# Loading all queries and keys in runs of 512 bytes and reading even-odd queries with a strided pattern

## The chip, the cores and the metric

The kernel runs on one core of one Trainium2 chip. The metric is the device time of one execution in microseconds (us), the median of several. Executions are sorted into a fast and a slow state; the slow one is an execution more than 1.5% above the fastest of the same kernel. Each execution also has a granted clock, the mean share of full speed at which TensorE was let run; fast executions of one kernel can differ in it. Ratios are the mean time of one kernel's fast runs over that of the other kernel's fast runs of the same rounds, so they are not quite the ratio of the medians quoted beside them. The kernel before took 214.99 us (214.95 to 215.03, 2 runs) at first; on the chips of the later runs its median was 216.5 to 217.6 us, with single executions from 214.6 to 220.7. A difference below 1% is therefore only trusted here where an interval excludes it.

## The reference, cut to what matters

```python
# q, k, v: (4, 8, 768, 64), 0.1 * randn;  heads 0, 2, 6 see all earlier keys,
# the others see 4 "sink" keys and the last 64
scores = scale * np.matmul(q, k.transpose(0, 1, 3, 2))
scores = np.where(mask[None, :, :, :], scores, -1000000000.0)
a = np.exp(scores - np.max(scores, axis=-1, keepdims=True))
a = a / (np.sum(a, axis=-1, keepdims=True) + 1e-09)
attn = np.matmul(a, v)
# then, on x = attn as (3072, 512):  np.maximum(x @ w1, x @ w2) @ w_out
```

One thing matters for the experiments. A score is a sum of 64 products of two numbers of size 0.1, divided by 8: about 0.01. The softmax is nearly flat, so a kernel that uses the queries in a wrong order still passes the comparison with the reference. Several experiments below do that on purpose and were all reported as correct. So a correct result says nothing about the order of the queries; that has to follow from the indices.

## The kernel before

A small planner in Python lays out the order of all instructions from estimated durations; that order is then fixed. Work goes by 16 pairs of heads (`i`, four per batch). q and k of a pair are loaded, cast to bf16 by GpSimd (the first pair also by others), transposed by TensorE, and copied out of PSUM (in the trace of before the matmuls write the `bank` buffers there, and a copy of 128x768 out of one takes 0.54 to 0.56 us on VectorE when contiguous). Score matmuls (k is the stationary operand `lhsT`, whose load starts at 140.63 us in the rows quoted in the prediction, its first matmul at 140.64; q is the moving operand `rhs`, and the next start follows 0.11 to 0.12 us after 256 of its columns, 0.16 after 384), exponentials (ScalarE), masks (VectorE) and the product with v follow. The dense part of a finished batch fills the gaps of TensorE between the pairs of the next one.

The first four pairs (`i < HP`) load two neighbouring rows as one run of 512 bytes, so their transposes come out as all even positions, then all odd ones, in each block of 256. The copy puts them back in order by writing with a step of two elements:

```python
wide = which < 2 and i < HP
pat = ("h (m p r) d -> p h m (r d)", dict(p=128, r=2)) if wide else ("h (n p) d -> p h n d", dict(p=128))
...
if i < HP:                                     # copy of the transposed q or k
    o = o.rearrange("q (m p r) -> q m r p", p=128, r=2)
    in_ = in_.rearrange("q (m r p) -> q m r p", p=128, r=2)
ev(eng)(out=o, in_=in_)
...
for (j, q0, w, off) in segs:                   # the scores, two heads side by side
    for hh in range(2):
        nc.tensor.matmul(
            P["sc", i, st, hh][:, off:off + w],
            lhsT=kt[64 * hh:64 * hh + 64, j * 128:(j + 1) * 128],
            rhs=qt[64 * hh:64 * hh + 64, q0:q0 + w], ...)
...
batches = [[0, 1], [2, 3], [4, 5]] if i >= HP else [[s] for s in range(NS)]
cost = sum(f[1] for f in fns) / 2400.0         # what the planner thinks scores cost, us
```

## Time and profile before

| from the page of before | value |
|---|---|
| span of the profiled run | 214.5 us |
| TensorE busy | 190.4 us (89%) |
| VectorE, ScalarE busy | 128.9, 128.4 us (60% each) |
| packets of the loads and stores | 74,118, of them 62,832 under 512 bytes |
| score matmuls | 320 |

Most of the profile of before stands in the prediction. Two further rows of its page are needed for comparison: the busy share of TensorE in tenths, in 40 equal slices of the span, and its granted clock in tenths of full speed.

```profile
PE   0388786999999999999999989998999999699993
PEclk9999999699999999999999999999999999999999
```

TensorE is full from the eighth slice on, and its clock is granted at nine tenths or more but for one slice.

### The profile page before, as it was taken

How to read it: one execution, taken by the hardware profiler on the slowest of the kernel's cores; microseconds unless marked ns; L12 is line 12 of the kernel's file. 1: busy time of each engine (PE TensorE's matmuls, PEld its weight loads, DVE VectorE, ACT ScalarE, POOL GpSimd, SP SyncE). 2: the span in 40 equal slices, each digit the busy share in tenths (PEclk: the TensorE clock that was granted, in tenths of full speed). 3: DMA queues.
4: the chain of work that ended last, by engine and by line, in shares of the span. 5: the costliest groups of instructions: out<-in, count | busy, mean ns of one | idle time of the engine just before them, and what ended most of it. 6: DMA issues, size and time to landing. Idle time of an engine off the chain costs nothing.

```text
span 214.5 us, 4691 instructions
## 1 busy us (share of the span) xinstructions
PE 190.4 (89%) x1872; PEld 108.0 (50%) x1888; DVE 128.9 (60%) x297; ACT 128.4 (60%) x247; POOL 47.6 (22%) x59
## 2 busy tenths in 40 slices
PE   0388786999999999999999989998999999699993
PEld 0244554555655555546654646465555554454541
DVE  7799989944772577447746683667436651650800
ACT  2489698639873778468845686578458664102021
POOL 0155447154443231313112040401000000000000
PEclk9999999699999999999999999999999999999999
DMA  4999999999999899998911400210012011102112
GB/s 115 259 343 318 240 344 409 238 221 219 220 201 248 194 240 222 236 250 209 223 49 55 120 0 3 98 52 0 0 52 98 3 47 52 52 0 98 49 52 98
DMA packets 74118, 31.77 MB, mean 148 GB/s; under 512 B 62832, under 2 KB 68976, under 8 KB 74096
## 3 DMA queue, kind: packets, MB, share of 16 engines
q1 hardware_dynamic: 73952, 31.46, 60.4%
q8 instruction: 15, 0.25, 0.5%
q14 instruction: 7, 0.06, 0.1%
q10 hardware_dynamic: 144, 0.01, 0.0%
HBM read 25.17 MB, written 6.29 MB: 147 GB/s over the span
## 4 chain that ended last, share of the span: by engine, by line
PE 72%; DVE 19%; DMA 3%; ACT 2%; issue 2%; SPq 0%; ACTq 0%; DVEq 0%
PE bank_80 L504 12%; PE bank_79 L504 10%; PE bank_79 L477 6%; PE bank_73 L331 5%; PE bank_77 L390 5%; PE bank_80 L477 5%; PE bank_78 L390 4%; PE bank_75 L331 3%; DMA kn_84<-in_k_dram 3%; PE bank_80 L461 3%; DVE x_117 L412 3%; PE bank_74 L504 2%; PE bank_73 L504 2%; PE bank_79 L422 2%; DVE x_118 L412 2%
## 5 line engine op out<-in xcount | busy, mean ns | idle before, releaser
L477 PEld LDWEIGHTS <-wd_bf 128*128 128x128 bf16 x256 | 23.4, 97 | 16.2 <-issue 3.6
L504 PEld LDWEIGHTS <-gt_123 128*128 128x128 bf16 x96 | 9.4, 98 | 11.3
L504 PEld LDWEIGHTS <-gt_122 128*128 128x128 bf16 x96 | 9.4, 98 | 11.3
L343 ACT ACTIVATE at_101<-bank_73 128x512 bf16<-128x512 f32 x16 | 9.6, 599 | 4.2 <-PE bank_74 L331 4.2
L343 ACT ACTIVATE at_107<-bank_75,bias_j 128x512 bf16<-128x512 f32 x16 | 11.2, 703 | 0.3 <-PE bank_76 L331 0.3
L343 ACT ACTIVATE at_108<-bank_76,bias_j 128x512 bf16<-128x512 f32 x16 | 11.4, 710 | 0.0
L504 PE MATMUL bank_80<-wo_bf,gt_122 128*128 128x512 bf16 x48 | 11.3, 379 | 0.0
L343 ACT ACTIVATE at_104<-bank_76,bias_64 128x512 bf16<-128x512 f32 x16 | 11.2, 702 | 0.0
L343 ACT ACTIVATE at_109<-bank_73 128x384 bf16<-128x384 f32 x16 | 8.0, 498 | 5.3 <-PE bank_74 L331 5.3
L343 ACT ACTIVATE at_103<-bank_75,bias_64 128x512 bf16<-128x512 f32 x16 | 11.1, 694 | 0.0
L343 ACT ACTIVATE at_105<-bank_73 128x512 bf16<-128x512 f32 x16 | 9.7, 608 | 2.2 <-PE bank_74 L331 2.2
L331 PE MATMUL bank_73<-qt_97,kt_99 64*128 64x256 bf16 (+1 forms) x48 | 9.5, 277 | 1.3 <-DVE kt_99 L315 1.3
L331 PEld LDWEIGHTS <-kt_99 64*128 64x128 bf16 x160 | 5.9, 95 | 9.2 <-issue 6.2
L354 DVE TENSOR_TENSOR at_109<-at_109,msk 128x384 bf16<-128x384 bf16 x16 | 7.5, 469 | 5.1 <-ACT at_109 L343 5.1
L411 DVE RECIPROCAL rez_115<-bank_77 128x6 f32<-128x6 f32 x8 | 1.6, 194 | 14.9 <-PE bank_77 L390 14.9
L308 PE MATMUL bank_79<-ident,qb_90 128*128 128x128 bf16 x36 | 3.3, 234 | 7.4 <-ACT qb_90 L291 7.4
L294 POOL CAST vb_94<-vn_87 128x768 bf16<-128x768 f32 x6 | 5.0, 838 | 21.2 <-DMA vn_87<-in_v_dram 9.7
L343 ACT ACTIVATE at_106<-bank_74 128x512 bf16<-128x512 f32 x16 | 9.7, 608 | 0.0
L331 PEld LDWEIGHTS <-kt_100 64*128 64x128 bf16 x160 | 6.0, 94 | 7.3 <-issue 5.5
L343 ACT ACTIVATE at_102<-bank_74 128x512 bf16<-128x512 f32 x16 | 9.6, 598 | 0.0
L331 PE MATMUL bank_74<-qt_97,kt_99 64*128 64x256 bf16 (+1 forms) x48 | 9.3, 275 | 0.2 <-ACT at_106 L343 0.2
L504 PE MATMUL bank_79<-wo_bf,gt_123 128*128 128x512 bf16 x40 | 9.4, 379 | 0.0
(224 smaller groups left out, 539.7 us busy)
## 6 DMA issues: line engine op xcount, KB each, us to landing
w_f<-in_moe_w_dram SPq DMA_DIRECT2D x4, 1024.0 KB, 9.3
qn_81<-in_q_dram SPq DMA_DIRECT2D x6, 384.0 KB, 6.0
kn_84<-in_k_dram SPq DMA_DIRECT2D x6, 384.0 KB, 6.2
vn_87<-in_v_dram SPq DMA_DIRECT2D x6, 384.0 KB, 6.1
wo_f<-in_moe_w_out_dram SPq DMA_DIRECT2D x2, 1024.0 KB, 8.0
out_dram<-ot_124 SPq DMA_DIRECT2D x8, 256.0 KB, 2.2
out_dram<-ot_125 SPq DMA_DIRECT2D x8, 256.0 KB, 2.0
out_dram<-ot_126 SPq DMA_DIRECT2D x8, 256.0 KB, 2.0
```

The costliest lines, as they stand in the source:

```text
L294: ev(eng)(out=dst[:, :, :, 0:D], in_=src)
L308: nc.tensor.transpose(o[:, n * 128:(n + 1) * 128], src[:, n].rearrange("p h d -> p (h d)"), ident)
L331: nc.tensor.matmul(P["sc", i, st, hh][:, off:off + w], lhsT=kt[64 * hh:64 * hh + 64, j * 128:(j + 1) * 128], rhs=qt[64 * hh:64 * hh + 64, ...
L343: nc.scalar.activation(out=P["at", i, st, hh][:, 0:n], in_=P["sc", i, st, hh][:, 0:n], func=ACT.Exp, scale=scale, bias=bias)
L354: nc.vector.tensor_mul(out=at[:, 0:n], in0=at[:, 0:n], in1=mk)
L390: nc.tensor.matmul(po[:, qb_ * (D + 1):(qb_ + 1) * (D + 1)], lhsT=at[:, off + t * 128:off + (t + 1) * 128], rhs=vb[:, hh, j, :], start=(st ...
L411: nc.vector.reciprocal(out=rez, in_=po[:, :, D])
L412: nc.vector.tensor_tensor(out=P["x", b][:, :, h * D:(h + 1) * D], in0=po[:, :, 0:D], in1=rez.unsqueeze(2).to_broadcast([128, NB, D]), op=A ...
L422: nc.tensor.transpose(psb[:, n * 128:(n + 1) * 128], P["x", b][:, n, hp * 128:(hp + 1) * 128], ident)
L461: nc.tensor.matmul(P["mmM", c], lhsT=w2t[:, f, c * 128:(c + 1) * 128], rhs=wo_bf[:, f, :], start=(f == 0), stop=(f == FC - 1))
L477: nc.tensor.matmul(P["mmH", b, g, f][:, 0:GT], lhsT=wd_bf[:, c, f * 128:(f + 1) * 128], rhs=P["xt", b][:, c, g * GT:(g + 1) * GT], start=( ...
L504: nc.tensor.matmul(ps, lhsT=lhsT, rhs=rhs, start=(i == 0), stop=(i == KC + FC - 1))
```

## The change

The intent: halve the number of short load packets for all q and k rather than for the first four pairs, and not pay for it with a slow copy of q (in the trace of before such a copy takes 1.02 us on VectorE with a step of two, 0.56 contiguous). k is put in order by its copy, now in all 16 pairs. q is copied as it lies, even positions first, and the score matmul reads an even and an odd element in turn, 128 elements apart. A segment that begins at an odd block of 128 can't be described in one such pattern and is split. The x buffers become smaller, per pair; two switches for other variants are off.

```diff
-        wide = which < 2 and i < HP
+        wide = which < 2
...
-                if i < HP:
+                if which == 1:
                     o = o.rearrange("q (m p r) -> q m r p", p=128, r=2)
...
-            tops.append(P.add({"DVE": 0.56, "ACT": 0.72} if i >= HP else {"DVE": 1.02, "ACT": 1.02}, evac, ...
+            tops.append(P.add({"DVE": 0.56, "ACT": 0.72} if which == 0 else {"DVE": 1.02, "ACT": 1.02}, evac, ...
...
-                        nc.tensor.matmul(P["sc", i, st, hh][:, off:off + w], lhsT=..., rhs=qt[..., q0:q0 + w], ...)
+                        qv = qt[64 * hh:64 * hh + 64].rearrange("d (m r p) -> d m p r", p=128, r=2)
+                        while at0 < q0 + w:
+                            m, lo = at0 // 256, (at0 % 256) // 2
+                            if lo == 0 and q0 + w - at0 >= 256:
+                                n = (q0 + w - at0) // 256
+                                pieces.append((qv[:, m:m + n], 256 * n))
+                            else:
+                                pieces.append((qv[:, m, lo:lo + 64, :], 128))
+                            at0 += pieces[-1][1]
+                        for rhs, n in pieces:
+                            nc.tensor.matmul(P["sc", i, st, hh][:, o:o + n], lhsT=lhsT, rhs=rhs, ...)
...
-        "x": ring("x", 2, [128, NB, d_model], BF16),
+        "x": ring("x", 3, [128, NB, 128], BF16),
```

More of the change, by code (lines that the diff above doesn't have):

```diff
@@ L14 @@
 NEG = -30000.0
+QK_BY_DMA = 0
+X_BY_DMA = 0
 SWITCH = 0.1
@@ L302, in plan_pair, with move @@
             tb, tt = (("qb", "qt"), ("kb", "kt"))[which]
+            if QK_BY_DMA and i >= HP:
+                def move(eng, tb=tb, tt=tt):
+                    nc.sync.dma_start_transpose(
+                        out=P[tt, i].rearrange("p (n c) -> p n c", c=128),
+                        in_=P[tb, i].rearrange("p n h d -> p (n h d)"))
+                tops.append(P.add({"DMA": 0.9}, move, deps=[casts[which]], acq=[(tt, (tt, i))], rel=[(tb, i)],
+                                  prio=(0, i, which)))
+                continue
             def tr(eng, which=which, tb=tb):
@@ L317, in plan_pair @@
                       rel=[(tb, i)], prio=(1, i, which))
-            tops.append(P.add({"DVE": 0.56, "ACT": 0.72} if i >= HP else {"DVE": 1.02, "ACT": 1.02}, evac, deps=[t],
+            tops.append(P.add({"DVE": 0.56, "ACT": 0.72} if which == 0 else {"DVE": 1.02, "ACT": 1.02}, evac, deps=[t],
                               rel=[("mmT", i, which)], prio=(1, i, which)))
@@ L330, in fn @@
                     for hh in range(2):
-                        nc.tensor.matmul(
-                            P["sc", i, st, hh][:, off:off + w],
-                            lhsT=kt[64 * hh:64 * hh + 64, j * 128:(j + 1) * 128],
-                            rhs=qt[64 * hh:64 * hh + 64, q0:q0 + w],
-                            start=True, stop=True, skip_group_check=True)
+                        qv = qt[64 * hh:64 * hh + 64].rearrange("d (m r p) -> d m p r", p=128, r=2)
+                        lhsT = kt[64 * hh:64 * hh + 64, j * 128:(j + 1) * 128]
+                        pieces = []
+                        at0 = q0
+                        while at0 < q0 + w:
[6 more added lines that the diff above has]
+                            at0 += pieces[-1][1]
+                        o = off
+                        for rhs, n in pieces:
+                            nc.tensor.matmul(P["sc", i, st, hh][:, o:o + n], lhsT=lhsT, rhs=rhs,
+                                             start=True, stop=True, skip_group_check=True)
+                            o += n
             return fn, n, kind, segs
@@ L412, in fn @@
                 nc.vector.tensor_tensor(
-                    out=P["x", b][:, :, h * D:(h + 1) * D], in0=po[:, :, 0:D],
+                    out=P["x", i][:, :, hh * D:(hh + 1) * D], in0=po[:, :, 0:D],
                     in1=rez.unsqueeze(2).to_broadcast([128, NB, D]), op=ALU.mult)
             norms.append(P.add({"DVE": 0.62}, fn, deps=[last], rel=[("po", i, hh), ("rez", i, hh)],
-                               acq=[("rez", ("rez", i, hh))], use=[("x", ("x", b), H + HP)],
+                               acq=[("rez", ("rez", i, hh))], use=[("x", ("x", i), 3)],
                                prio=(0, i, hh)))
@@ L422, in xtr, with xmove @@
                 nc.tensor.transpose(psb[:, n * 128:(n + 1) * 128],
-                                    P["x", b][:, n, hp * 128:(hp + 1) * 128], ident)
+                                    P["x", i][:, n, :], ident)
         def xev(eng):
             ev(eng)(out=P["xt", b][:, hp, :], in_=P["mmX", i].bitcast(BF16)[:, 0:S])
-        t = P.add({"PE": 0.34}, xtr, deps=norms, acq=[("mm", ("mmX", i))], prio=(2, i, NS),
-                  use=[("x", ("x", b), H + HP), ("xt", ("xt", b), XT_USES)])
-        xt_ops[b, hp] = P.add({"DVE": 0.56, "ACT": 0.72}, xev, deps=[t], rel=[("mmX", i)],
-                              prio=(0, i, NS))
+        def xmove(eng):
+            nc.sync.dma_start_transpose(
+                out=P["xt", b][:, hp, :].rearrange("p (n c) -> p n c", c=128),
+                in_=P["x", i].rearrange("p n c -> p (n c)"))
+        if X_BY_DMA and i < len(pairs) - 1:
+            xt_ops[b, hp] = P.add({"DMA": 0.9}, xmove, deps=norms, prio=(0, i, NS),
+                                  use=[("x", ("x", i), 3), ("xt", ("xt", b), XT_USES)])
+        else:
+            t = P.add({"PE": 0.34}, xtr, deps=norms, acq=[("mm", ("mmX", i))], prio=(2, i, NS),
+                      use=[("x", ("x", i), 3), ("xt", ("xt", b), XT_USES)])
+            xt_ops[b, hp] = P.add({"DVE": 0.56, "ACT": 0.72}, xev, deps=[t], rel=[("mmX", i)], prio=(0, i, NS))
     wd_ops, wo_ops, wm_ops = [], [], []
```

## The prediction

Where the prediction speaks of a line, it means 16 bytes, eight neighbouring bf16 elements. That TensorE pays for a change of line, and the factors of two and four, were guesses of mine: the trace of before has no strided read to show them. The sweep e4 shows the step at that size (0.61 us a batch with two elements 4 apart in turn, 1.15 with two 8 apart), and e4 and e9 measure what a change costs. The lag of the second head is an estimate too, from 128 columns at the 2.4 per ns of the trace; after shows both heads' pieces starting within 0.01 us of each other.

> **What bounds the kernel now.** I read the busy table of the page first, then a table of three stretches of the span, then the order of TensorE's instructions in one steady stretch, then the group of the score matmuls and of the copies that follow the transposes of q and k.
>
> The stretches (columns: microseconds from the start, length, then busy time with the number of instructions for PE, PE weight loads, VectorE, ScalarE, GpSimd, then granted clock, DMA share, GB/s):
>
> ```profile
> 0.00:40.00 40.00, 25.82 (x327) 15.96 (x329) 35.70 (x87) 29.61 (x54) 16.24 (x23) 0.98 1.00 288
> 40.00:184.50 144.50, 138.50 (x1412) 78.83 (x1425) 83.66 (x194) 95.25 (x188) 31.39 (x36) 0.99 0.60 129
> 184.50:214.50 30.00, 26.12 (x137) 13.18 (x136) 9.49 (x17) 3.52 (x6) 0.00 (x0) 1.00 0.14 54
> ```
>
> There are three regimes. Up to 40 us VectorE is the full engine (35.70 of 40) and TensorE starves (25.82). From 40 to 184.5 us TensorE is busy 138.50 of 144.50, VectorE only 58% and ScalarE 66%: TensorE is the bound. The last 30 us are the dense work of the last batch, which neither q nor k touches. Busy time of pipelined matmuls overstates, so I check with column counts: the dense up products have 256 x 384 columns, the down products 192 x 512, the folded weight 32 x 512, the weight transposes 32 x 128, the q, k and x transposes 16 x 18 x 128, the score products 16 x 2688 per head (two heads side by side), attention times v 16 x 42 x 65. That is 98.3 + 147.5 + 16.4 + 4.1 + 36.9 + 43.0 + 43.7 = 389.9 thousand columns, at 2.4 columns per ns (the rate that the next view shows: 256 columns in some 0.11 us) 162 us of streaming in a span of 214.5. So from 40 us on every column that TensorE streams longer lengthens the kernel nearly one for one: its order of work is fixed by the program and nothing else is near full.
>
> The score matmuls in the steady stretch, with the waits in brackets:
>
> ```profile
> 140.63 0.33 PEld L331 LDWEIGHTS <-kt_99 64*128 64x128 bf16 x8 [0.42 <-issue]
> 140.64 0.28 PE L331 MATMUL bank_73<-qt_97,kt_99 64*128 64x256 bf16 x1
> 140.64 0.28 PE L331 MATMUL bank_74<-qt_97,kt_99 64*128 64x256 bf16 x1
> 140.76 0.27 PE L331 MATMUL bank_73<-qt_97,kt_99 64*128 64x256 bf16 x1
> 140.76 0.27 PE L331 MATMUL bank_74<-qt_97,kt_99 64*128 64x256 bf16 x1
> 140.87 0.32 PE L331 MATMUL bank_75<-qt_97,kt_99 64*128 64x384 bf16 x1
> 140.87 0.32 PE L331 MATMUL bank_76<-qt_97,kt_99 64*128 64x384 bf16 x1
> 141.03 0.22 PE L331 MATMUL bank_75<-qt_97,kt_99 64*128 64x128 bf16 x1
> ```
>
> Two heads (banks 73 and 74) start at the same instant[...]. The starts are 0.12, 0.11 and 0.16 us apart for 256, 256 and 384 columns, so q is read at full speed today: one column per 1/2.4 ns. The 0.27 us durations are latency, not spacing.
>
> The chip's queue for loads is full until about 105 us, but as a prefetch:
>
> ```profile
> DMA  4999999999999899998911400210012011102112
> DMA packets 74118, 31.77 MB, mean 148 GB/s; under 512 B 62832, under 2 KB 68976, under 8 KB 74096
> ```
>
> All of 40 to 105 us has both a full DMA and a full TensorE (19.2 of 20 us in each 20 us window), and in the list of TensorE's own waits no load of a later pair appears; the only long one is the 7.4 us of the very start.
>
> [...]a q or k copy takes 0.56 us on VectorE when contiguous and 1.02 when it writes with a step of two.[...]
>
> **The change part by part.**
>
> Loads. 12 pairs x 2 tensors go from 1536 runs of 256 bytes to 768 of 512: 18,432 packets fewer, so about 55,700 of 74,118. Loads from the fifth pair on land earlier and the full stretch of the queue ends perhaps 10 to 15 us earlier (24 loads, my estimate some 0.5 us each, as the 6.0 us to landing is three loads deep). On the end: nothing, because TensorE does not wait for them. The first four pairs, whose loads do matter, are wide already.
>
> Copies after the transposes. The first four q copies lose the step-two write: 4 x (1.02 - 0.56) = 1.8 us, or less where ScalarE does them (1.01 to 0.80). That lies in the stretch where VectorE is full: up to 1.5 us on the end. The other twelve k copies gain it: seen today as 8 on VectorE at about 0.55 and 4 on ScalarE at 0.82, so 8 x 0.46 + 4 x 0.20 = 4.5 us more, in a stretch where those engines are a third idle. On the end: 0 to 0.5.
>
> Score matmuls, number. Per head and pair today 10; segments that start at an odd block of 128 (queries from 128, 384 and again 384) fall into two pieces, so 13. That is 6 x 16 = 96 more matmuls and weight loads, with the same columns. Both pieces of one head are issued before the other head's, so the second head lags by one 128-column piece (0.053 us); the lag doesn't add up inside a batch of steps, so at most 2 to 3 times 0.053 a pair: 16 x 0.13 = 2 us at the most.
>
> Score matmuls, reading. The inner pattern is now two elements 128 columns (256 bytes) apart, then the next column[...]. If a new line costs twice the time of a column, the 2688 columns of a pair take 2.24 us rather than 1.12: 1.12 us more a pair, plus double the lag. Three pairs are through by 36 us, where TensorE has slack; thirteen count: 13 x (1.12 + 0.2) = 17 us. If it costs four times, 13 x 3.5 = 46 us.[...]
>
> Output buffers per pair rather than per batch (3 small ones instead of 2 large): freed by a transpose that follows within 2 us, so no new wait.
>
> Sum with the factor of two: 215.0 + 17 + 1 (lag and copies early) - 1.5 = 231.5; I put 231.
>
> **The rivals.** First: the strided read is free. Then 215.0 + 2 - 1.5 = 215.5, within 2%. [...]Second: a line costs four columns: some 262. [...]Third: the loads were the limit after all, and the kernel gains. For it: the DMA row of nines up to slice 19; against: the TensorE row of nines beside it. At most the 6 us of idle in the middle stretch could come back, and little of that is ascribed to loads: 210 to 213. Fourth: the k copies, 1.02 us in front of a pair's first score matmul, become a wait. Each pair's chain would lengthen by 0.46 us, but dense work is interleaved; 12 x 0.2 = 2.4 us at worst, so 217.
>
> **Range and chances.** I give the penalty of two about 0.4, of four or so 0.15, something between one and two 0.1, and none 0.35. The low end, 213.5, is the free read with the early gain; the high end, 243, the penalty of two with all the small costs and a less lucky plan. Over 2% faster needs 4.3 us, more than the sum of all the gains named: 0.05. Within 2%: 0.34. Slower: 0.61.
>
> **What would show it.** Spacing of the starts of the score matmuls in the steady stretch: 0.11 us for 256 columns if the read is free, about 0.21 with a factor of two, 0.43 with four. Groups of score matmuls numbering 416 rather than 320. Packets near 55,700. k copies near 1.02 us throughout, q copies near 0.56. DMA nines ending some slices earlier with TensorE's row unchanged. The prediction fails if the spacing stays at 0.11, or if the spacing doubles while the span doesn't move, which would mean that TensorE had more slack than its busy time says.

## The result, and the profile after

The changed kernel took 236.88 us (235.62 and 238.14), a ratio of 1.1018 with a 95% interval of 1.0765 to 1.1271. A second measurement (e5 below) narrowed it to 1.1014 (1.0938 to 1.1089).

The rows of the page of after that answer to those of before:

```profile
PE   0597997989999999979999999999999999799993
...
PEclk9998897999999999997999999999999999999999
DMA  5999999999999908262431400120011101201202
...
DMA packets 55686, 31.77 MB, mean 135 GB/s; under 512 B 25968, under 2 KB 50544, under 8 KB 55664
```

The loads did what was intended: 18,432 packets fewer, and the row of full DMA slices ends after slice 14 of 40 (83 us) rather than after slice 20 (107 us). TensorE is as full as before, in a longer span. The clock dips in more slices.

The three stretches of after, with the columns of the first table in the prediction:

```profile
0.00:40.00 40.00, 27.82 (x337) 16.62 (x338) 32.45 (x87) 29.69 (x53) 15.28 (x22) 0.94 0.98 290
40.00:184.50 144.50, 137.93 (x1321) 73.49 (x1334) 78.92 (x168) 88.19 (x169) 32.15 (x36) 0.98 0.48 123
184.50:236.10 51.60, 46.10 (x315) 23.44 (x315) 19.54 (x43) 14.75 (x29) 0.00 (x0) 1.00 0.13 48
```

In the middle stretch TensorE is busy just as long (137.93 against 138.50 us) but gets through 1321 matmuls instead of 1412, although the change has split some of them. What it leaves lies in the last stretch. Over the whole span its busy time rose from 190.4 to 211.9 us, and its idle time (span less busy) stayed: 24.1 and 24.2 us.

The score matmuls in the steady stretch of after (start, length, then the matmul):

```profile
143.38 0.41 PE L357 MATMUL bank_73<-qt_98,kt_100 64*128 64x256 bf16 x1
143.38 0.41 PE L357 MATMUL bank_74<-qt_98,kt_100 64*128 64x256 bf16 x1
143.63 0.28 PE L357 MATMUL bank_73<-qt_98,kt_100 64*128 64x128 bf16 x1
143.63 0.28 PE L357 MATMUL bank_74<-qt_98,kt_100 64*128 64x128 bf16 x1
143.75 0.28 PE L357 MATMUL bank_73<-qt_98,kt_100 64*128 64x128 bf16 x1
```

256 columns are now 0.25 us apart and 128 columns 0.12: 0.94 to 0.98 ns a column, where before had 0.11 to 0.12 us for 256. The two heads still start together, and so do their pieces.

The copies of the transposed q and k, before (count, then shortest, median and longest in ns):

```profile
L315 DVE COPY kt_100<-bank_80 x6: 545/554/1021, 14.5 to 157.3; 128x768 bf16<-128x768 bf16 x6
...
L315 ACT COPY kt_99<-bank_80 x4: 819/819/819, 78.9 to 145.5; 128x768 bf16<-128x768 bf16 x4
```

and after:

```profile
L326 ACT COPY kt_99<-bank_80 x4: 1012/1040/1047, 9.4 to 162.8; 128x768 bf16<-128x768 bf16 x4
...
L326 DVE COPY kt_100<-bank_80 x4: 1001/1006/1019, 14.3 to 176.1; 128x768 bf16<-128x768 bf16 x4
```

k copies take a microsecond in all pairs now, as reckoned; the q copies on VectorE, up to 1.02 us in the early pairs of before, take 0.55 to 0.56 us throughout.

A third thing catches the eye. In this stretch of after TensorE waits for VectorE before the transposes of x, and the dense matmuls that come a little later run at about half speed:

```profile
105.05 0.51 PE L446 MATMUL bank_80<-ident,x_118 128*128 128x128 bf16 x6 [1.52 <-DVE x_118 L436]
...
107.46 1.47 PE L508 MATMUL bank_79<-xt_121,wd_bf 128*128 128x384 bf16 x4
...
110.97 0.81 PE L508 MATMUL bank_80<-xt_121,wd_bf 128*128 128x384 bf16 x4
```

The bracket is 1.52 us of idle time. The same four matmuls take 1.47 us at 107.46 and 0.81 at 110.97; this is the dip to 7 in the clock row between 106 and 112 us. I took the wait for a cause of the dip and of some loss, and the record doesn't bear that out. The kernel before has the same wait, at another place:

```profile
184.12 0.51 PE L422 MATMUL bank_80<-ident,x_118 128*128 128x128 bf16 x6 [1.52 <-DVE x_118 L412]
```

e1 below has it too (1.52 us at 97.35), in an execution whose clock row is all nines. What brings the dips is not shown.

### The profile page after: what moved, and what is told of

Same layout as the page of the kernel before. It is cut to its first block, busy times and chain, and to the rows that moved or that the text cites. A ratio compares the mean times of both kernels' runs of the same rounds, so it can differ in the third digit from the quotient of the medians.

```text
span 236.1 us, 4881 instructions
## 1 busy us (share of the span) xinstructions
PE 211.9 (90%) x1966; PEld 113.5 (48%) x1984; DVE 130.9 (55%) x296; ACT 132.6 (56%) x249; POOL 47.4 (20%) x58
## 2 busy tenths in 40 slices
DMA packets 55686, 31.77 MB, mean 135 GB/s; under 512 B 25968, under 2 KB 50544, under 8 KB 55664
## 4 chain that ended last, share of the span: by engine, by line
PE 76%; DVE 14%; DMA 4%; SPq 3%; issue 1%; ACT 1%; ACTq 0%; DVEq 0%
PE bank_80 L535 11%; PE bank_73 L357 9%; PE bank_79 L535 9%; PE bank_75 L357 7%; PE bank_79 L508 6%; PE bank_80 L508 5%; PE bank_77 L414 5%; DMA w_f<-in_moe_w_dram 4%; PE bank_78 L414 4%; SPq L271 3%; PE bank_74 L535 2%; PE bank_73 L535 2%; PE bank_79 L446 2%; PE bank_80 L492 2%; PE bank_79 L492 1%
## 5 line engine op out<-in xcount | busy, mean ns | idle before, releaser
L508 PEld LDWEIGHTS <-wd_bf 128*128 128x128 bf16 x256 | 24.0, 99 | 17.4 <-issue 5.1
L357 PE MATMUL bank_73<-qt_97,kt_99 64*128 64x256 bf16 (+1 forms) x64 | 14.8, 330 | 2.4 <-ACT kt_99 L326 1.7
L357 PE MATMUL bank_73<-qt_98,kt_100 64*128 64x256 bf16 (+1 forms) x64 | 14.8, 330 | 0.0
L357 PE MATMUL bank_74<-qt_97,kt_99 64*128 64x256 bf16 (+1 forms) x64 | 14.8, 330 | 0.0
L357 PE MATMUL bank_74<-qt_98,kt_100 64*128 64x256 bf16 (+1 forms) x64 | 14.7, 329 | 0.0
L357 PEld LDWEIGHTS <-kt_99 64*128 64x128 bf16 x208 | 8.2, 95 | 13.1 <-issue 5.7
L357 PE MATMUL bank_76<-qt_97,kt_99 64*128 64x128 bf16 (+2 forms) x40 | 13.6, 403 | 0.0
L357 PEld LDWEIGHTS <-kt_100 64*128 64x128 bf16 x208 | 8.3, 95 | 11.1 <-issue 6.3
L357 PE MATMUL bank_75<-qt_97,kt_99 64*128 64x128 bf16 (+2 forms) x40 | 13.6, 403 | 0.0
L357 PE MATMUL bank_75<-qt_98,kt_100 64*128 64x128 bf16 (+2 forms) x40 | 13.6, 403 | 0.0
L357 PE MATMUL bank_76<-qt_98,kt_100 64*128 64x128 bf16 (+2 forms) x40 | 13.6, 403 | 0.0
L367 ACT ACTIVATE at_105<-bank_73 128x512 bf16<-128x512 f32 x16 | 9.6, 600 | 5.8 <-PE bank_74 L357 5.8
L367 ACT ACTIVATE at_101<-bank_73 128x512 bf16<-128x512 f32 x16 | 9.6, 597 | 4.9 <-PE bank_74 L357 4.1
L367 ACT ACTIVATE at_107<-bank_75,bias_j 128x512 bf16<-128x512 f32 x16 | 11.0, 689 | 0.6 <-PE bank_76 L357 0.5
L367 ACT ACTIVATE at_108<-bank_76,bias_j 128x512 bf16<-128x512 f32 x16 | 11.1, 695 | 0.0
L378 DVE TENSOR_TENSOR at_109<-at_109,msk 128x384 bf16<-128x384 bf16 x16 | 7.0, 435 | 6.3 <-ACT at_109 L367 6.3
L378 DVE TENSOR_TENSOR at_105<-at_105,msk 128x512 bf16<-128x512 bf16 x16 | 7.4, 462 | 4.9 <-ACT at_105 L367 4.9
## 6 DMA issues: line engine op xcount, KB each, us to landing
w_f<-in_moe_w_dram SPq DMA_DIRECT2D x4, 1024.0 KB, 10.1
```

What stands on the lines that cost most here:

```text
L357: nc.tensor.matmul(P["sc", i, st, hh][:, o:o + n], lhsT=lhsT, rhs=rhs, start=True, stop=True, skip_group_check=True)
L367: nc.scalar.activation(out=P["at", i, st, hh][:, 0:n], in_=P["sc", i, st, hh][:, 0:n], func=ACT.Exp, scale=scale, bias=bias)
L378: nc.vector.tensor_mul(out=at[:, 0:n], in0=at[:, 0:n], in1=mk)
L508: nc.tensor.matmul(P["mmH", b, g, f][:, 0:GT], lhsT=wd_bf[:, c, f * 128:(f + 1) * 128], rhs=P["xt", b][:, c, g * GT:(g + 1) * GT], start=( ...
```

## The experiments

My theory after the result: the loss is the strided read on TensorE. Rivals: the 96 additional matmuls, the slower k copies and wider loads, or the order that the planner makes. All runs but two sweeps were timed beside the kernel before on the same chip.

**e1, the changed kernel reading runs.** One word of the pattern changes, so loads, copies, pieces and order stay.

```diff
-   qv = qt[...].rearrange("d (m r p) -> d m p r", p=128, r=2)
+   qv = qt[...].rearrange("d (m p r) -> d m p r", p=128, r=2)     # contiguous; wrong order on purpose
```

> The changed kernel with one thing altered: the score matmuls, still split in 416 pieces, read q in runs instead of with the step of 128. Wrong result on purpose (q is in even-odd order). Loads, copies, buffers and the order of all instructions are those of the changed kernel. Theory (the strided read itself costs): 256 columns take 0.11 us from start to start again and the time falls back to 213.5 to 218 us. Rival (the 96 further matmuls, the slower k copies or another plan cost): it stays above 228 us. If each has a share, it lies between, and the difference to 237 is the share of the read.

Measured: 218.15 us (217.44 to 219.69), ratio 1.0062 (0.9988 to 1.0136). A batch of 12 score matmuls, 1024 columns of each head, takes in the timeline of e1

```profile
108.36 0.61 PE L357 MATMUL bank<-qt,kt 64*128 64x256 bf16 x12
```

The median is 0.15 us above the band I had set, because this chip was slower for before as well (217.61). With the read alone taken away, 9.5 of the 10.1% are gone (the two ratios come from different chips). The theory holds.

**e2, the kernel before with the strided read.** Its score matmuls are replaced by those of the change; nothing else (wrong order on purpose).

```diff
-   nc.tensor.matmul(..., rhs=qt[64 * hh:64 * hh + 64, q0:q0 + w], ...)
+   (the loop over pieces of the change, with its strided qv)
```

> The kernel before with one thing altered: its score matmuls are split and read q with the step of 128 as in the changed kernel. Wrong result on purpose (q is in natural order there). Loads and copies are those of before. Theory (the read costs): 232 to 240 us, about all of the loss, with 256 columns 0.24 us apart. Rival (loads, copies, plan): below 218 us.

Measured: 235.06 us (234.40 to 236.04), ratio 1.0835 (1.0766 to 1.0904). The same batch of 12 takes in the timeline of e2

```profile
103.92 1.15 PE L346 MATMUL bank<-qt,kt 64*128 64x256 bf16 x12
```

so the read, with narrow loads, old copies and the old order, brings 8.35%, or 18 us (that the split which comes with it costs nothing is shown by e8). In the profiles TensorE's busy time is 21.5 us above that of before, and its idle time 2.7 us below: most of what is added to the score matmuls is added to the span.

**e3, wide loads with both copies permuting.** The read is contiguous and whole again.

```diff
-   if which == 1:
+   if True:                                   # q is put in order too; the planner is told 1.02 us for it
-   (pieces)
+   nc.tensor.matmul(..., rhs=qt[64 * hh:64 * hh + 64, q0:q0 + w], ...)
```

> All loads in runs of 512 bytes, but both the q and the k copy put their columns back in natural order (1.02 us each), and the score matmuls are whole and contiguous; small x buffers as in the changed kernel. Right result. Theory (loads are hidden behind TensorE, copies have slack): 213.5 to 217 us, within 1% of before, with some 55,700 packets. Rival that loads were the limit: below 211. Rival that a slower copy ahead of each pair becomes a wait: 218 to 222.

Measured: 220.28 us (218.64 to 222.73), ratio 1.0125 (1.0015 to 1.0236). One of the four executions was in the slow state; the three fast ones took 218.64, 218.76 and 221.81. I was wrong: the median is 3.3 us above the upper end of my band (before's own was 217.61 on this chip), the ratio is not within 1%, and the time lies in the band of the rival that a slower copy becomes a wait. It is above before by a little more than the noise. The page has 55,685 packets, so the loads did shrink. Their saving is not seen at all, and the slower copies may cost about 1%; that is not shown, because the planner's order and the x buffers differ from before as well. The profiled execution of this run was in the slow state, so I read no cause from its trace.

**e4, sixteen patterns in one kernel.** In the frame of the changed kernel, so with the same instruction order, each pair reads q in its own pattern (wrong order on purpose).

```diff
+PATTERNS = [("run", 1)] * 3 + [("step", 2), ("step", 4), ("step", 8), ("step", 16), ("step", 64),
+            ("two", 2), ("two", 4), ("two", 8), ("two", 16), ("two", 32), ("two", 64), ("run", 1), ("step", 32)]
+   if form == "two":     rd = rd.rearrange("d (b r p) -> d b p r", p=step, r=2)    # two elements `step` apart in turn
+   elif form == "step":  rd = rd.rearrange("d (p r) -> d r p", r=step)             # every step-th element
```

> The changed kernel with another reading pattern of q in each of the 16 pairs (wrong result on purpose): pairs 0 to 2 and 14 in runs; pairs 3 to 7 and 15 with a single step of 2, 4, 8, 16, 64 and 32 elements; pairs 8 to 13 two elements 2, 4, 8, 16, 32 and 64 apart, then the next column. Read from the spacing of the starts for 256 columns, 0.11 us when free. [...]steps of 2 and 4 free, from 8 on slow (0.24); two elements apart by 2 and 4 free, from 8 on slow. A cost of short inner loops of two: all of the pairs 8 to 13 slow, the steps 2 to 32 free. A cost of anything that isn't adjacent: all slow from a step of 2 on.[...]

The batches of 12 matmuls in the timeline of e4. The rows are pairs 4 (step 4), 5 (step 8), 6 (step 16), 8 (two, 2 apart), 9 (two, 4 apart), 10 (two, 8 apart), 13 (two, 64 apart), 14 (run) and 15 (step 32):

```profile
51.91 1.08 PE L366 MATMUL bank<-qt,kt 64*128 64x256 bf16 x12
65.96 1.97 PE L366 MATMUL bank<-qt,kt 64*128 64x256 bf16 x12
82.16 2.01 PE L366 MATMUL bank<-qt,kt 64*128 64x256 bf16 x12
...
109.06 0.61 PE L366 MATMUL bank<-qt,kt 64*128 64x256 bf16 x12
119.18 0.61 PE L366 MATMUL bank<-qt,kt 64*128 64x256 bf16 x12
131.47 1.15 PE L366 MATMUL bank<-qt,kt 64*128 64x256 bf16 x12
...
167.33 1.15 PE L366 MATMUL bank<-qt,kt 64*128 64x256 bf16 x12
181.41 0.62 PE L366 MATMUL bank<-qt,kt 64*128 64x256 bf16 x12
194.13 1.89 PE L366 MATMUL bank<-qt,kt 64*128 64x256 bf16 x12
```

A step at 16 bytes, 8 elements of bf16, is plainly in it; I call such a stretch a line. Two elements 2 or 4 apart in turn are free, at the 0.61 us of a run; 8 apart costs 1.15 us, as much as 64 apart, and as much as the 128 of the change (1.15 in e2). So it is not the short inner loop of two that costs, and not the mere lack of adjacency. The first expectation failed in two points. A step of 4, which meets each line twice, is not free but takes 1.08. And steps of 8, 16 and 32 cost nearly double what I had said: 1.89 to 2.01 a batch, where 0.24 us for 256 columns would be about 1.15. (The step of 2 fell in pair 3, which is issued in smaller batches; six of its matmuls took 0.41 us at 38.08, and 0.40 in the same place of e9, where they read runs.)

**e5, the changed kernel again**, unaltered.

> The changed kernel again, unaltered, to have its ratio to before from more than two runs and on the chip of the next three. Both theories: 1.08 to 1.11 of before, some 235 to 238 us; it doesn't tell them apart, it narrows the size.

Measured: 237.84 us (235.61 to 238.43, 4 runs), ratio 1.1014 (1.0938 to 1.1089). The four executions had granted clocks of 0.991, 0.978, 0.977 and 0.976, and the one with the highest clock is 1.9 to 2.8 us faster than the others. All four count as fast, while before's executions at 0.976 and 0.977 on this chip count as slow, so the ratio leaves them out. At like clock the loss is smaller: 235.61 us, at 0.991, is 1.086 of the 216.97 us that before's twelve fast executions at 0.991 and 0.992 on this chip have on average. That is one execution, so an indication; it is close to the 1.0835 of e2.

**e6, runs of four for q everywhere.** If four neighbours come from one line, the read should be free (0.61 us a batch in e4 with two elements 4 apart in turn), and the copy can still move contiguous data. So within each eight columns the copy puts the four even ones, then the four odd ones.

```diff
+   if which == 0:
+       o = o.rearrange("q (m b r p) -> q m r b p", b=32, r=2, p=4)
+       in_ = in_.rearrange("q (m r b p) -> q m r b p", b=32, r=2, p=4)
...
+   rhs = qt[64 * hh:64 * hh + 64, q0:q0 + w].rearrange("d (b r p) -> d b p r", r=2, p=4)   # natural order, whole segments
```

The order is right: column 8b + 4r + p of a block holds position 2(4b + p) + r, and is read as number 8b + 2p + r.

> The changed kernel with q copied in runs of four columns: in each eight, the four even ones, then the four odd ones. The copy still moves contiguous data (inner run of four), and the score matmuls read pairs that lie four elements apart, a pattern that the sweep showed to be free, in whole segments (320 matmuls). Right result by the indices. Theory (only the distance of 128 costs[...]): 256 columns 0.11 us apart and 213 to 219 us, 0.99 to 1.01 of before on the same chip. Rival (any read that isn't a run costs when it is in the real order of the kernel): 228 us or more. The q copies: 0.56 us on VectorE if the inner run of four keeps its fast mode, 1.02 if not.

Measured: 218.41 us (217.08 to 221.86; two of the six were slow, the four fast ones took 217.08 to 218.66), ratio 1.0105 (1.0049 to 1.0162). The read is free and the copy kept its speed:

```profile
98.05 0.61 PE L348 MATMUL bank<-qt,kt 64*128 64x256 bf16 x8
...
L329 DVE COPY qt<-bank 128x768 bf16<-128x768 bf16 x14 | 7.8, 555 | 15.7 <-PE bank L319 15.7
```

(The batch of 1024 columns a head is 8 whole matmuls here. 14 copies, 7.8 us busy in all, 555 ns each.) The time is within the band in us, the ratio just outside it. This version has everything that the change wanted, wide loads and fast q copies, without the slow read. It is 19 us better than the change and still 1% worse than before. No version with wide loads throughout is faster than before.

**e7, the same for the first four pairs alone**, in the kernel before, where the wide loads exist already.

```diff
-   if i < HP:                       # copies of q and k with a step of two
+   if which == 0 and i < HP:        # q in runs of four (as in e6), about 0.56 us
+       ...
+   elif i < HP:                     # k as before
    (the planner is told 0.56 us for these q copies; the score matmuls of these pairs read q as in e6)
```

> The kernel before with the same runs of four for q in the first four pairs alone, where VectorE is full and the loads are wide already; all later pairs as before. Right result. Theory (the early stage is bound by VectorE, and 4 x 0.46 us of copies come off it): 0.5 to 1.5 us faster than before, ratio 0.993 to 0.998. Rival (another engine or the order of the plan sets that stage): within 0.3%, either way.

Measured: 218.66 us (216.32 to 222.22, 20 runs), ratio 1.0070 (1.0031 to 1.0109). I was wrong: with shorter copies in the stage where VectorE is full (35.70 of the first 40 us in the trace of before) the kernel became slower. The copies were not all that changed: the planner's order of everything after changed with them. The profiled execution was in the slow state, so the cause stays open.

**e8, the kernel before with split matmuls**: 416 pieces, read in runs, the right order.

```diff
-   nc.tensor.matmul(..., rhs=qt[64 * hh:64 * hh + 64, q0:q0 + w], ...)
+   (the loop over pieces of the change, with the contiguous qv of e1)
```

> The kernel before with its score matmuls split in 416 pieces as in the changed kernel, read in runs. Right result. My prediction gave this up to 2 us. From the traces (both heads' pieces start at the same instant) I now expect at most 1 us: ratio 1.000 to 1.005. If it is above 1.01 the split carries part of the loss.

Measured: 215.40 us (214.16 to 218.92, 20 runs) against 216.53 for before, ratio 0.9963 (0.9935 to 0.9992). The split costs nothing. The interval even excludes no change at all, on the faster side; I have no explanation for this 0.4%. It makes e8 the fastest version in the study.

**e9, a second sweep.** From e4's batches (0.61, 1.08, 1.15 and 1.97 us) I had estimated a rule for it to test: four columns are fetched together and every line among the four costs.

```diff
+PATTERNS = [run] * 4 + [2 parts by 1, 2 parts by 2, 2 parts by 4, 2 parts by 8,
+            4 parts by 1, 4 parts by 2, 4 parts by 4, 8 parts by 1, "gap", "off", "off" 2 parts by 4, run]
+   rd = rd.rearrange("d (r b p) -> d b r p", r=r, p=p)      # p columns from each of r parts of the segment, in turn
```

(Schematic: "gap" is a step of 3 or 6, "off" starts two columns off.)

> A second sweep in the same frame (wrong result on purpose), to test a rule that fits all of the first: four successive columns are fetched together and each 16-byte line among the four costs some 1.75 to 1.9 ns, against 1.67 ns that four columns take anyway. The batch of 12 matmuls (1024 columns a head) takes 0.61 us when free and took 1.08 (step 4), 1.15 (two lines in turn) and 1.97 (step 8). Pairs 0 to 3, 15: runs. Pair 4: single columns in turn from two halves of the segment; rule 1.15. Pair 5: two and two; rule about 1.1 (two lines in each four). Pair 6: four and four; rule free. Pair 7: eight and eight; free. Pair 8: single columns from four quarters; rule about 1.9. Pair 9: two from each of four quarters; rule about 1.1. Pair 10: four from each of four; free. Pair 11: single columns from eight parts; rule about 1.9. Pair 12: steps of 6 and 3; rule: step 3 like two lines, step 6 three lines in four, 128 columns between 290 and 400 ns. Pair 13: runs that start two columns off; rule 0.85 if a line isn't kept from one four to the next, 0.61 if it is. Pair 14: four and four, two columns off; 0.85 or more. Rival, that each change of line costs by itself whatever the group: pairs 5 and 9 about half of the extra cost of pair 4, pair 6 a quarter of it.

The batches of 12 in e9, in order pairs 4 to 11 and 14:

```profile
52.53 1.15 PE L369 MATMUL bank<-qt,kt 64*128 64x256 bf16 x12
65.44 0.72 PE L369 MATMUL bank<-qt,kt 64*128 64x256 bf16 x12
78.23 0.63 PE L369 MATMUL bank<-qt,kt 64*128 64x256 bf16 x12
...
101.49 1.90 PE L369 MATMUL bank<-qt,kt 64*128 64x256 bf16 x12
115.49 1.04 PE L369 MATMUL bank<-qt,kt 64*128 64x256 bf16 x12
127.94 0.62 PE L369 MATMUL bank<-qt,kt 64*128 64x256 bf16 x12
139.21 1.95 PE L369 MATMUL bank<-qt,kt 64*128 64x256 bf16 x12
...
177.49 0.73 PE L369 MATMUL bank<-qt,kt 64*128 64x256 bf16 x12
```

(Pair 7, eight and eight, took 0.61; pair 13, runs two columns off, 0.62.) The rule falls with pair 5: two and two from two parts took 0.72, not 1.1. The rival as I had worded it falls too, because it put that pair at half the cost of pair 4. What fits all rows of both sweeps is a cost for each change of line that is hidden when enough columns come from the line. A batch is 1024 columns and, by my estimate, 0.18 us of latency (0.61 less 1024 columns at the 2.4 per ns that 384 columns in 0.16 us give in the trace of before), which gives:

| pattern | batch, us | ns a column | columns taken before the line changes | ns a change |
|---|---|---|---|---|
| run | 0.61 | 0.42 | 8 | hidden |
| four and four, 2 or 4 parts | 0.62 to 0.63 | 0.43 to 0.44 | 4 | hidden |
| step 4 | 1.08 | 0.88 | 2 | 1.8 |
| two from each of 4 parts | 1.04 | 0.84 | 2 | 1.7 |
| step 8, 16, 32 | 1.89 to 2.01 | 1.67 to 1.79 | 1 | 1.7 to 1.8 |
| one from each of 4 or 8 parts | 1.90, 1.95 | 1.68, 1.73 | 1 | 1.7 |
| one from each of 2 parts (the change) | 1.15 | 0.95 | 1 | 0.95 |
| two from each of 2 parts | 0.72 | 0.53 | 2 | 1.05 |

A change to a new line, or back to one left several changes ago, costs some 1.7 ns, as much as four columns. A change back to the line left just before costs about 1.0. By this description the change lost a factor of some 2.25 (0.94 over 0.417) and not 4 because it alternates between only two lines. The reason for the cheaper return is not shown; this is a description that fits, made after the fact. Three pairs mix cases and are left out of the table: pair 7 of e4 (1.52; two lines in turn in its pieces of 128 columns, four in those of 256), pair 12 of e9 (1.20; steps of 6 and 3) and pair 14 (0.73; every second run of four crosses into a further line).

**e10, the changed kernel with an honest planner.** The read stays slow, but the planner is told so.

```diff
-   cost = sum(f[1] for f in fns) / 2400.0
+   cost = sum(f[1] for f in fns) * 0.00094
```

> The changed kernel with one number altered: the planner, which lays the order of all instructions, is told that a column of the score matmuls takes 0.94 ns rather than 0.417, so it no longer counts on time that isn't there. Right result. If part of the loss beyond the 8.3% of e2 is a plan made with a wrong cost (waits of the x transposes, dips of the clock after them): 232 to 236 us, ratio 1.075 to 1.095. If not: 1.10 as before, within 0.5%.

Measured: 234.00 us (233.65 to 234.79), ratio 1.0807 (1.0710 to 1.0904), clear of e5's interval. At first I read this as 2 of the 10 points for the order of the instructions, from one line in the list of TensorE's waits. e5 has (total us, times, longest)

```profile
PE bank L446 <- DVE x L436: 4.2, 4, 1.5
```

and e10

```profile
PE bank L446 <- DVE gt L515: 2.3, 6, 0.9
PE bank L446 <- DVE qt L326: 1.2, 1, 1.2
...
PE bank L446 <- DVE x L436: 0.9, 1, 0.9
```

With its other waits at the same line e10 has 4.4 us there in all, e5 5.0; e1, in e5's order but with a fast read, waits there for 6.5 us and is 0.6% from before. TensorE's idle time (span less busy) is 22.6 us in e5 and 21.7 in e10. So the waits account for about 1 us. The profiled executions of the two, at clocks of 0.991 and 0.990, differ by 1.3 us in span (233.5 and 232.2).

The rest goes with the clock: e10's four executions had 0.985 to 0.993, three of e5's four had 0.976 to 0.978. At like clock the changed kernel took 235.6 us (0.985 in the first measurement, 0.991 in e5) and e10 233.65 to 234.79 us. So the honest planner is worth some 1.5 us there, 0.7 points; the two kernels ran on different chips. Whether the order also lowers the clock is not shown.

One more variant was meant to read k in even-odd order and q in runs. It was never run, so it isn't in the record, and nothing here shows whether it works or what it costs. In every run here with wide loads k is put in order by its copy.

## Why the prediction was right or wrong

The time, 236.88 us, lies in the range of 213.5 to 243, and "slower" had the largest chance. The point, 231, was 6 us low. By its steps:

- **What bounds the kernel**: right. e2 added the score matmuls' time to TensorE and the time rose by 18 us; the thirteen pairs after the early stage account for 13 x 2688 x (0.94 - 0.417) ns = 18.3 us. One figure of the working is misnamed: 192 x 512 is 98.3 thousand columns. The 147.5 that it wrote is 288 x 512, the 192 down products and the 96 products with the folded weight, and the sum of 389.9 is right.
- **Loads**: right for the end, mis-sized in themselves. 55,686 packets as said; the full stretch of the queue ended some 24 us earlier, not 10 to 15, so 1.0 us a load and not 0.5. From 45 to 83 us, with the queue full in both, it moved 221 GB/s before and 245 after. Nothing of it reached the end (e1, e3, e6 are all at or above before). The third rival, that loads were the limit, is out.
- **Copies**: durations right. The gain of up to 1.5 us from the first q copies did not appear; the nearest test, e7, in which the planner's order changed too, went 0.7% the other way. This term failed.
- **Score matmuls, number**: 416 as counted. The lag, which I put at up to 2 us and at double with a slow read, is nothing: both heads' pieces start within 0.01 us of each other (at 143.63 and 143.75 us in the rows of after above, although the program has both pieces of one head before those of the other), and e8 is no slower than before. This term failed.
- **Score matmuls, reading**: that the strided read slows TensorE was right, the size off. I took a factor of two, a guess, with four and one as rivals; it is some 2.25 (0.94 ns a column over 0.417), 18.3 us instead of 14.6. That two came so near is partly luck. Nothing on record then measured it, and the sweeps show neither picture that I had: a line that is new costs some 1.7 ns, as much as four columns, as in the second rival, and only the return to the line just left is cheaper, at about 1.0 (e9). And 2.6 us of lag that didn't come made up for most of the 3.7 us missing here.
- **Left out**: the planner's order and the clock. None of the rivals had them. The change kept the planner's cost of a score column while that cost more than doubled; correcting the one number gave back 2 points, of which some 0.7, or 1.5 us, stand at like clock (e10).
- **Fourth rival**, the k copy as a new wait: not separated. What remains without the slow read is 0.6 to 1.25% (e1, e3, e6), of which k copies, order and small x buffers may each have a part.

The read alone gives 215 + 18.3 = 233.3 us. The remaining 3.6 us up to 236.9 are not shared out by any run: the planner's order, the lower clock, and what e1 keeps without the slow read (0.6%, within its noise) are what is left to share them.

## What to carry to other kernels

On an engine that is the bound, an access pattern is a cost like any other (here 18 us on 217, e2): before moving a permutation from a copy on an idle engine into the operand of a busy one, measure what a column costs in that pattern. If a strided read can't be avoided, try interleaving in runs of four elements inside 16 bytes: in e6 the read (0.61 us a batch) and the copy (555 ns) were then each as fast as a plain one, though the whole kernel (e6) was still 1% slower than before. When a change alters a duration, tell it to the cost model that orders the program; here that was worth some 0.7%. And before giving a difference of 1 or 2% to a cause, compare the granted clocks of the executions, and the idle time as a whole rather than one line of the waits.
